# Linear attention and a rational feed-forward layer on one core: attention by pairs of blocks, the state in half-block steps, a newly planned order

## The chip, the core and the metric

The kernel runs on one core of a Trainium2 chip. A core has five engines with a queue of their own each: TensorE (PE in the profile; its weight loads are listed as PEld), VectorE (DVE), ScalarE (ACT), GpSimd (POOL) and SyncE (SP), which here issues the DMA transfers. TensorE writes into PSUM; VectorE and ScalarE read PSUM and SBUF; GpSimd's operands here are all in SBUF. The metric is the device time of one execution in microseconds (us).

## The reference

A recurrence over 768 time steps in 4 batches and 8 heads of width 48, and behind it a feed-forward layer with a rational activation:

```python
for t in range(S):                       # r, k, v: (4, 8, 768, 48)
    cur = einsum('bhd,bhe->bhde', u[None] * k[:, :, t], v[:, :, t])
    y[:, :, t] = einsum('bhd,bhde->bhe', r[:, :, t], state + cur)
    state = w[None, :, :, None] * state + einsum('bhd,bhe->bhde', k[:, :, t], v[:, :, t])
h = x @ w_in                             # x: y as (3072, 384); w_in: (384, 2048)
P = a[0] + a[1]*h + a[2]*h*h + a[3]*h*h*h
Q = 1.0 + abs(b[0])*abs(h) + abs(b[1])*h*h
out = (P / (Q + 1e-6)) @ w_out           # w_out: (2048, 384)
```

## The kernel before

**Attention** is done in 24 blocks of 128 time steps (block n is batch n % 4, steps 128 (n // 4) and on). The decay is divided out: r is scaled by powers of w, k by their inverses (scale_r, scale_k), so that inside a half block of 64 steps the recurrence is a masked product. A block takes these steps. The bonus of the current step is formed by elementwise multiplies and a sum (bonus_a, bonus_b, bonus_sum, bonus_v). k and r are transposed on TensorE (trk_pe, trr_pe, line 415) and copied out of PSUM. a_pe (lines 438 and 439) makes, for each pair of heads p and each half e, two 64x64 products, one from the array's rows 0 to 63 into columns 64 to 127, one from rows 64 to 127 into columns 0 to 63: 16 matmuls a block, all into one PSUM bank. a_ev masks them (line 452). kv_pe (lines 472 and 473) forms the sums of k times v: for the first half block alone over 64 rows, and for both halves together over 128 rows. kv_ev (line 487) adds each to the state carried in, and carry (line 511) decays the state for the next block of the batch. y_pe (line 500) multiplies the r rows and the masked a rows with the state and v rows, 128 rows deep, in two column halves. y_ev adds the bonus, xt_pe (line 519) transposes the result, and xt_hi and xt_lo split it into a high part and a rest.

**The feed-forward layer** works on 12 tiles of two blocks (256 rows). Both weights are split into a high part and a rest once (28 pieces, cv_load to cv_lo, which use ScalarE, VectorE and GpSimd). A product of two split numbers is three matmuls. A tile has eight slices of two 128-column groups of the hidden layer: f1 (mm, line 541) makes 18 matmuls of 256 columns; ew_z, ew_q, ew_t, ew_ln, ew_exp on ScalarE (lines 572 to 592) and ew_u3, ew_hi, ew_p, ew_d, ew_lo on VectorE (lines 596 to 616) give the activation, split again in g: a high part (ew_hi) and a rest (ew_lo); f2 (mm2, lines 545 to 547) makes 12 matmuls of 384 columns. With the last slice cut in two there are 97. The second matmul of a slice waits for ew_lo.

**The order** of every engine's instructions is written out before the program starts. Every step is a task with the engines that may do it, a duration, its dependences, the buffers it takes and a key; run() plays the queues through with these durations, and each time an engine comes free it gives it the ready task with the smallest key. Loads of k, r and v aren't issued before their own time on this clock (AT of the block, less some us). Where TensorE has nothing ready early on, it gets small matmuls on ones (warm, line 1009). Two parameters settle where ew_lo runs: GTIME = 754.72 is the time from which GpSimd may have it, which never comes, so it stays on VectorE; by the same bound the masking stays on VectorE. The planned order is fixed; on the chip each instruction waits for what it needs, and whatever stands behind it on its engine waits too.

Of the kernel before, what the change touches and what calls it, by code (L numbers as in the profile page):

```python
# [30 lines left out]


@with_exitstack
def tile_linear_attention_rational_ffn(ctx, tc, r, k, v, w, u, w_in, w_out, a, b, out):
# [15 lines left out]
    NM = 7  # L50
    NTC = 2
# [32 lines left out]
    w128b = w128.unsqueeze(2).to_broadcast([P, NP, D])  # L84
# [236 lines left out]
    rh, kh, ysa, ysb, vs = ([], [], [], [], [])  # L321
    vs2 = [cst.tile([P, 5, 2, NP, D], F32, name=f"vs{i}") for i in range(B // 2)]
    for i in range(3):
        for lst, nm in ((rh, "rh"), (kh, "kh")):
            lst.append(cst.tile([P, NP, 2, HALF], F32, name=f"{nm}{i}"))
    kt = cst.tile([P, NP, P], F32, name="kt")
    for i in range(2):
        for lst, nm in ((ysa, "ysa"), (ysb, "ysb")):
            lst.append(cst.tile([P, NP, P], F32, name=f"{nm}{i}"))
# [4 lines left out]
    def pro_pad(i):  # L334
        for lst in (rh, kh):
            nc.gpsimd.memset(lst[i][:, :, :, D:HALF], 0.0)

# [16 lines left out]
    def att_load(n, what):  # L354
        bi, i = blk(n)
        c = slice(i * P, (i + 1) * P)
        if what == "v":
            t, src = ld.tile([P, H, D], F32, tag="ldv", name=f"vn{n}"), v
            state[n]["v"] = t
        else:  # L360
            t, src = (hv(kh[n % 3]), k) if what == "k" else (hv(rh[n % 3]), r)
        nc.sync.dma_start(t, src[bi, :, c, :].rearrange("h t d -> t h d"))
# [27 lines left out]
    def scale_r(n, e):  # L390
        rr = hv(rh[n % 3])
        e.tensor_mul(rr, rr, wrn)

    def bonus_a(n, e):
        m = at.tile([P, H, D], F32, tag="m", name=f"m{n}", bufs=NM)
        e.tensor_mul(m, hv(rh[n % 3]), hv(kh[n % 3]))
# [15 lines left out]
    def trans(n, src, nm):  # L412
        p_ = pat(nm, n)
        for p in range(NP):
            nc.tensor.transpose(p_[:, ts(p, P)], src[:, p].rearrange("t a d -> t (a d)"), ident)  # L415
# [5 lines left out]
    def trk_ev(n, e):  # L421
        copy(e, kt.rearrange("p a t -> p (a t)"), state[n]["tk"])

    def trr_pe(n):
        trans(n, rh[n % 3], "tr")

    def trr_ev(n, e, half):
        y_, rows = ((ysa, slice(0, HALF)), (ysb, slice(HALF, P)))[half]
        copy(e, y_[n % 2][rows].rearrange("p a t -> p (a t)"), state[n]["tr"][rows])

    def a_pe(n):
        p_ = pat("a", n)
        ya, yb = ysa[n % 2], ysb[n % 2]
        for p in range(NP):
            for e in range(2):
                c = slice(e * HALF, (e + 1) * HALF)
                o = slice(p * P + e * HALF, p * P + (e + 1) * HALF)
                nc.tensor.matmul(p_[HALF:P, o], kt[0:HALF, p, c], ya[0:HALF, p, c], start=True, stop=True)  # L438
                nc.tensor.matmul(p_[0:HALF, o], kt[HALF:P, p, c], yb[HALF:P, p, c], start=True, stop=True)
        state[n]["a"] = p_  # L440

    def a_rows(n, half):
        return ((ysa[n % 2], slice(HALF, P)), (ysb[n % 2], slice(0, HALF)))[half]


    def a_ev(n, half, e):
        y_, rows = a_rows(n, half)
        av = state[n]["a"][rows]
        if e is nc.scalar:
            copy(e, y_[rows].rearrange("p a t -> p (a t)"), av)  # L450
            return
        nc.vector.tensor_mul(
            y_[rows].rearrange("p a (e t) -> p (a e) t", e=2), av.rearrange("p (c t) -> p c t", t=HALF),
            mask[rows].unsqueeze(1).to_broadcast([HALF, 2 * NP, HALF]),
        )

    def a_mask(n, half):
        y_, rows = a_rows(n, half)
        yv = y_[rows].rearrange("p a t -> p (a t)")
        nc.gpsimd.affine_select(  # L460
            yv, yv, pattern=[[0, 2 * NP], [1, HALF]], base=-1, channel_multiplier=-1,
            compare_op=ALU.is_ge, fill=0.0,
        )

    def kv_pe(n):
        d = state[n]
        p_ = pat("kv", n)
        k_, v_ = kh[n % 3], d["v"]
        pv = p_[:, 0 : 2 * NP * D].rearrange("p (e a d) -> p e a d", e=2, a=NP)
        for e, rows in ((0, slice(0, HALF)), (1, slice(0, P))):  # L470
            for p in range(NP):
                nc.tensor.matmul(pv[0:D, e, p], k_[rows, p, 0, 0:D], v_[rows, 2 * p], start=True, stop=True)  # L472
                nc.tensor.matmul(
                    pv[HALF : HALF + D, 1 - e, p], k_[rows, p, 1, 0:D], v_[rows, 2 * p + 1], start=True, stop=True
                )
        d["kv"] = pv

    def kv_ev(n, e, half):
        bi, i = blk(n)
        s_, pv = vs[bi], state[n]["kv"]  # L480
        outs, prev, rows = ((slice(1, 3), 0, slice(0, D)), (slice(2, 5, 2), 3, slice(HALF, HALF + D)))[half]
        o = s_[rows, outs].rearrange("p e a d -> p e (a d)")
        kv = pv[rows].rearrange("p e a d -> p e (a d)")
        if i == 0:
            copy(e, o, kv)
        else:
            nc.vector.tensor_add(
                o, kv, s_[rows, prev : prev + 1].rearrange("p e a d -> p e (a d)").to_broadcast([D, 2, NP * D])
            )

    def y_pe(n):
# [4 lines left out]
        for p in range(NP):  # L496
            for x, (y_, S_) in enumerate(((ysa[n % 2], SA), (ysb[n % 2], SB))):
                for e in range(2):
                    c = slice(e * HALF, (e + 1) * HALF)
                    nc.tensor.matmul(pv[c, 2 * p + x], y_[:, p, c], s_[:, S_[e], p], start=True, stop=True)  # L500
# [6 lines left out]
    def carry(n, e, half):  # L507
        bi, i = blk(n)
        s_ = vs[bi]
        dst, rows = ((0, slice(0, D)), (3, slice(HALF, HALF + D)))[half]  # L510
        e.tensor_mul(s_[rows, dst], s_[rows, 2], w128b[rows])  # L511
# [32 lines left out]
    def mm2(o, j, hi, lo):  # L544
        nc.tensor.matmul(o, hi, wo_hi[:, j], start=(j == 0), stop=False)  # L545
        nc.tensor.matmul(o, hi, wo_lo[:, j], start=False, stop=False)  # L546
        nc.tensor.matmul(o, lo, wo_hi[:, j], start=False, stop=(j == NJ - 1))  # L547


    SL = [(f, j, JG) for f in range(NTILE) for j in range(0, NJ, JG)]  # L550
    SL[-1:] = [(NTILE - 1, j, 1) for j in range(NJ - JG, NJ)]
    NS = len(SL)

# [84 lines left out]
    def f2(s, hf):  # L638
        f, j0, nj = SL[s]
        if j0 == 0 and hf == 0:  # L640
            ops[f] = [ps_o.tile([P, 512], F32, tag=f"o{x}", name=f"o{f}_{x}") for x in range(2)]
        for jj in range(nj):
            c = ds(jj * N1 + hf * P, P)
            mm2(ops[f][hf][:, 0:DM], j0 + jj, gs[s]["hi"][:, c], gs[s]["lo"][:, c])

    def put_out(f, e, hf):
        bi, i = blk(2 * f + hf)
        os_ = at.tile([P, DM], F32, tag="os", name=f"os{f}_{hf}")
        if e is nc.scalar:
            e.activation(os_, ops[f][hf][:, 0:DM], AF.Copy, scale=SG)  # L650
        else:
            e.tensor_scalar(os_, ops[f][hf][:, 0:DM], SG, None, op0=ALU.mult)
        oss[f, hf] = os_

    def put_dma(f, hf):
# [478 lines left out]
```

## Time and profile before

| what | value |
|---|---|
| time of the runs | 595.18 us median of 3 (594.43 to 595.61) |
| profiled execution | span 593.4 us from its first to its last instruction; its own time is not listed beside the span |
| PE, PEld busy | 563.1 us (95%), 540.8 us (91%) |
| DVE busy | 517.7 us (87%) |
| ACT busy | 435.5 us (73%) |
| POOL busy | 166.5 us (28%) |
| matmuls of f1 (x1728), f2 (x1152) | lines 541; 545, 546 and 547 |
| clock-keeping matmuls | 514, 35.2 us |
| mean granted TensorE clock | 0.984 |

Matmuls overlap in a pipeline, so the duration of one (289 ns for f1's) is more than the time from one start to the next; what a matmul costs is read from the distance of the starts. A float32 matmul of attention shows as two records. The rows of the profile are: line, engine, operation, tiles written and read, shapes, count, then busy time and mean duration, then the idle time of the engine before these instructions and what ended it.

### The profile page before, as it was taken

Reading aid. Unit: us, or ns where it says so; the run is one execution under the profiler, and the core shown is the slowest. Engines: PE = TensorE matmul, PEld = TensorE weight load, DVE = VectorE, ACT = ScalarE, POOL = GpSimd, SP = SyncE. Lnnn points to the kernel's source line nnn. Section 1 sums busy time; section 2 is a strip of 40 time slices with the busy share of each in tenths; the row PEclk is TensorE's granted clock in tenths of the full one; section 3 lists DMA queues with packets and bytes.
Section 4 is the critical chain, followed back from the end, with each engine's and each line's share of the span. In section 5 each row is a group of like instructions: output and inputs, shape, how many; then the busy total and the mean of one; then the engine's idle time right before and its main releaser. Section 6 shows DMA issues by size and latency. Waiting matters only on the chain.

```text
span 593.4 us, 14638 instructions
## 1 busy us (share of the span) xinstructions
PE 563.1 (95%) x5991; PEld 540.8 (91%) x5991; DVE 517.7 (87%) x825; ACT 435.5 (73%) x729; POOL 166.5 (28%) x189
## 2 busy tenths in 40 slices
PE   8899696789999999999999999999999999999995
PEld 8799585778999999999999999999999999999995
DVE  5999998999999997889899888898888998888882
ACT  7679876978862785777677878865778785888780
POOL 6698976664135121013040010143001010000000
PEclk9999888989999999999999999999999999999999
DMA  7687653551222230012020003021003000000000
GB/s 189 163 224 193 166 142 92 127 109 32 55 53 57 68 75 8 2 41 54 28 55 2 27 1 73 10 42 43 14 0 81 2 15 15 0 28 2 28 1 31
DMA packets 95807, 34.85 MB, mean 59 GB/s; under 512 B 89074, under 2 KB 92148, under 8 KB 95732
## 3 DMA queue, kind: packets, MB, share of 16 engines
q1 hardware_dynamic: 95732, 33.83, 23.4%
q8 instruction: 49, 0.80, 0.6%
q14 instruction: 26, 0.21, 0.1%
HBM read 29.11 MB, written 4.72 MB: 57 GB/s over the span
## 4 chain that ended last, share of the span: by engine, by line
PE 71%; DVE 3%; ACT 1%; issue 1%
PE h L541 29%; PE o L545 11%; PE o L546 10%; PE o L547 10%; PE y L500 2%; PE a L438 2%; PE kv L472 2%; PE x L519 1%; PE tk L415 1%; PE tr L415 1%; DVE h L596 1%; DVE q L606 0%; DVE g L602 0%; DVE vs L511 0%; ACT t L583 0%
## 5 line engine op out<-in xcount | busy, mean ns | idle before, releaser
L541 PE MATMUL h<-xth,wi_hi 128*128 128x256 f32 x576 | 166.2, 289 | 0.0
L541 PE MATMUL h<-xtl,wi_hi 128*128 128x256 f32 x576 | 161.6, 281 | 0.0
L541 PE MATMUL h<-xth,wi_lo 128*128 128x256 f32 x576 | 161.5, 280 | 0.0
L545 PE MATMUL o<-wo_hi,g 128*128 128x384 f32 x384 | 134.8, 351 | 0.0
L547 PE MATMUL o<-wo_hi,g 128*128 128x384 f32 x384 | 130.4, 339 | 1.4 <-DVE g L616 1.4
L546 PE MATMUL o<-wo_lo,g 128*128 128x384 f32 x384 | 130.1, 339 | 0.0
L572 ACT ACTIVATE q<-h 128x512 f32<-128x512 f32 (+1 forms) x97 | 57.4, 591 | 83.3 <-PE h L541 63.0
L541 PEld LDWEIGHTS h<-xth,wi_hi 128*128 128x128 f32 x576 | 109.0, 189 | 1.2
L541 PEld LDWEIGHTS h<-xtl,wi_hi 128*128 128x128 f32 x576 | 109.2, 190 | 0.0
L541 PEld LDWEIGHTS h<-xth,wi_lo 128*128 128x128 f32 x576 | 108.8, 189 | 0.0
L602 DVE SCALAR_TENSOR_TENSOR g<-h,sig,z 128x512 fp32r<-128x512 f32 (+1 forms) x97 | 72.0, 743 | 28.1 <-ACT z L592 25.8
L578 ACT ACTIVATE w<-q,off,root 128x512 f32<-128x512 f32 (+1 forms) x97 | 75.8, 781 | 2.9 <-DVE q L606 2.7
L596 DVE SCALAR_TENSOR_TENSOR h<-t,sig,h 128x512 f32<-128x512 f32 (+1 forms) x97 | 72.0, 742 | 3.2 <-ACT t L583 2.9
L583 ACT ACTIVATE t<-h,off,root 128x512 f32<-128x512 f32 (+1 forms) x97 | 74.7, 770 | 0.1
L547 PEld LDWEIGHTS o<-wo_hi,g 128*128 128x128 f32 x384 | 72.6, 189 | 2.4 <-DVE g L616 2.4
L612 DVE SCALAR_TENSOR_TENSOR h<-h,sig,q 128x512 f32<-128x512 f32 (+1 forms) x97 | 72.7, 750 | 2.3
L606 DVE SCALAR_TENSOR_TENSOR q<-w,sig,g 128x512 f32<-128x512 f32 (+1 forms) x97 | 72.1, 743 | 2.6
L545 PEld LDWEIGHTS o<-wo_hi,g 128*128 128x128 f32 x384 | 72.6, 189 | 1.4
L546 PEld LDWEIGHTS o<-wo_lo,g 128*128 128x128 f32 x384 | 72.7, 189 | 0.0
L592 ACT ACTIVATE z<-z,lnb 128x512 f32<-128x512 f32 (+1 forms) x97 | 69.9, 721 | 2.3
L588 ACT ACTIVATE z<-w,lnb 128x512 f32<-128x512 f32 (+1 forms) x97 | 66.4, 685 | 3.6 <-POOL wi_lo L306 1.1
L616 DVE TENSOR_TENSOR g<-h,z 128x512 fp32r<-128x512 f32 (+1 forms) x97 | 65.7, 679 | 0.7
(147 smaller groups left out, 932.0 us busy)
## 6 DMA issues: line engine op xcount, KB each, us to landing
sto<-in_moe_w_out_dram SPq DMA_DIRECT2D x16, 384.0 KB, 3.7
sti<-in_moe_w_in_dram SPq DMA_DIRECT2D x12, 512.0 KB, 5.2
rh<-in_r_dram SPq DMA_DIRECT2D x24, 192.0 KB, 3.7
kh<-in_k_dram SPq DMA_DIRECT2D x24, 192.0 KB, 3.3
vn<-in_v_dram SPq DMA_DIRECT2D x24, 192.0 KB, 3.4
out_dram<-os SPq DMA_DIRECT2D x24, 192.0 KB, 1.9
vs<-in_v_dram SPq DMA_DIRECT2D x24, 96.0 KB, 3.5
wraw<-in_w_dram SPq DMA_DIRECT2D x1, 1.5 KB, 2.3
```

Of the source, the lines that this page charges most:

```text
L541: nc.tensor.matmul(o, wt_[:, cc, ts(j, P)], x_[:, cc], start=(n == 0), stop=(n == 3 * NCC - 1))
L545: nc.tensor.matmul(o, hi, wo_hi[:, j], start=(j == 0), stop=False)
L546: nc.tensor.matmul(o, hi, wo_lo[:, j], start=False, stop=False)
L547: nc.tensor.matmul(o, lo, wo_hi[:, j], start=False, stop=(j == NJ - 1))
L578: nc.scalar.activation(g["w"], w_, AF.Square, scale=RB, bias=KB)
L583: nc.scalar.activation(g["t"], g["h"], AF.Square, scale=RA, bias=KA)
L588: nc.scalar.activation(g["z"], g["w"], AF.Ln, scale=2.0 ** -LN_SHIFT, bias=lnb[:, 2:3])
L592: nc.scalar.activation(g["z"], g["z"], AF.Exp, scale=-1.0, bias=lnb[:, 1:2])
L596: nc.vector.scalar_tensor_tensor(g["h"], g["t"], KAP, g["h"], op0=ALU.add, op1=ALU.mult)
L602: nc.vector.scalar_tensor_tensor(g["hi"], g["h"], c0, g["z"], op0=ALU.add, op1=ALU.mult)
L606: nc.vector.scalar_tensor_tensor(g["q"], g.get("w", g["q"]), qe, g["hi"].bitcast(F32), op0=ALU.add, op1=ALU.mult)
L612: nc.vector.scalar_tensor_tensor(g["d"], g["h"], c0, g["q"], op0=ALU.add, op1=ALU.subtract)
```

## The change

- **a by pairs of blocks.** a_pe takes a pair of blocks (the same steps of two batches; one tile of the feed-forward layer). Its 32 matmuls are 48 rows deep, and consecutive ones go round all four 64x64 quadrants of the array: q, the head of the pair, chooses the rows, e, the half block, the columns. Each row half writes a PSUM bank of its own. The result is masked in four pieces per pair instead of two per block, with the same number of elements.
- **The state per half block in a chain.** kv_pe takes a pair too. Each half block has its own sum, 64 rows deep, in a quadrant; the state at the half block is the state carried in and the first sum, the state at the end is that and the second sum (kv_ev). The product over 128 rows is gone. For the last block of each batch the second sum isn't formed. carry is done once for a pair, over twice the elements.
- **Buffers.** kt and ys hold both blocks of a pair; r has two buffers instead of three; the rows between 48 and 64 of ys are cleared once (pro_rest).
- **The planner** moves out of the kernel to order_of, with a new set of keys and release times (PRM). It knows three modes of the array, a cost for switching between them (TURN) and a bonus MB for staying in one. The first matmul of a slice no longer names pieces of w_out as a dependence; f2 does. Clock-keeping matmuls may be set until 248.69 on its clock (60.0 before), but none after the first f2 has started.
- **The rest's multiply (ew_lo)** goes to GpSimd for the slices listed in SIDE, 20 to 96; ew_d then writes SBUF instead of PSUM for these.
- NT is 1, so the new code for several tiles in turn (NSEG, SEG, opens, closes, partial sums in put_out) leaves the order of slices as it was.

```diff
+PRM = {'AT': (19.16, 39.84, 50.08, 155.58, 173.74, 187.74, 196.43, 217.1, 298.25, 394.8, 423.47, 439.93),
...
+ 'DX': -15.2,
+ 'HFREE': 1,
+ 'MASKED': (),
+ 'MB': 6.1,
+ 'NT': 1,
...
+ 'SIDE': (20, 21, 22, 23, 24, 25, 26, 27, 28, 29, 30, 31, 32, 33, 34, 35, 36, 37, 38, 39, 40, 41, 42, 43, 44, 45, 46, 47, 48, 49,
...
+          80, 81, 82, 83, 84, 85, 86, 87, 88, 89, 90, 91, 92, 93, 94, 95, 96),
+ 'WARM0': 1.6,
+ 'WARM1': 248.69,
...
+TURN = {(0, 0): 0.0, (0, 1): 0.15, (0, 2): 0.15, (1, 0): 0.19, (2, 0): 0.19, (1, 2): 0.2, (2, 1): 0.2, (1, 1): 0.0, (2, 2): 0.0}
...
-    def a_pe(n):
-        p_ = pat("a", n)
-        ya, yb = ysa[n % 2], ysb[n % 2]
-        for p in range(NP):
-            for e in range(2):
-                c = slice(e * HALF, (e + 1) * HALF)
-                o = slice(p * P + e * HALF, p * P + (e + 1) * HALF)
-                nc.tensor.matmul(p_[HALF:P, o], kt[0:HALF, p, c], ya[0:HALF, p, c], start=True, stop=True)
-                nc.tensor.matmul(p_[0:HALF, o], kt[HALF:P, p, c], yb[HALF:P, p, c], start=True, stop=True)
+    def a_pe(m):
+        ps = [pat("a", (m, q)) for q in range(2)]
+        for x in range(2):
+            for p in range(NP):
+                for e in range(2):
+                    c = ts(e, HALF)
+                    for q in range(2):
+                        nc.tensor.matmul(
+                            ps[q][c, ts(x * NP + p, HALF)], kt[RROWS[q], x, p, c], ys[q][RROWS[q], x, p, c], start=True, stop=True
+                        )
...
-    def kv_pe(n):
-        for e, rows in ((0, slice(0, HALF)), (1, slice(0, P))):
...
-                nc.tensor.matmul(pv[0:D, e, p], k_[rows, p, 0, 0:D], v_[rows, 2 * p], start=True, stop=True)
+    def kv_pe(m):
+        last = m // 2 == NB - 1
+        ps = [pat("kv", (m, e)) for e in range(1 if last else 2)]
+        for x in range(2):
+            k_, v_ = hv(kh[(2 * m + x) % 3]), state[2 * m + x]["v"]
             for p in range(NP):
+                for e, p_ in enumerate(ps):
+                    for q in range(2):
+                        nc.tensor.matmul(
+                            p_[RROWS[q], ts(x * NP + p, D)], k_[ts(e, HALF), 2 * p + q], v_[ts(e, HALF), 2 * p + q], start=True, stop=True
+                        )
...
+    def kv_ev(m, q, e, on):
+        s_ = vs2[m % 2][RROWS[q]].rearrange("p e x a d -> p e (x a d)")
+        chain = ((0, 1, 2), (3, 4, 2))[q]
+        pv, dst = state["kv", m, e][RROWS[q]], s_[:, chain[e + 1]]
+        if m < 2 and e == 0:
+            copy(on, dst, pv)
         else:
+            nc.vector.tensor_add(dst, pv, s_[:, chain[e]])
...
+    def carry(m, q, e):
+        s_ = vs2[m % 2][RROWS[q]]
+        e.tensor_mul(s_[:, (0, 3)[q]], s_[:, 2], w128[RROWS[q]].unsqueeze(1).unsqueeze(3).to_broadcast([D, 2, NP, D]))
...
+                tx = t + x * PRM["DX"]
+                add(("Lk", n), lambda e, n=n: att_load(n, "k"), tx - 6, {"S": 1.2}, [w_("kv", (n - 3) // 2), w_("tk", n - 3), w_("ba", n - 3)])
+                add(("Lr", n), lambda e, n=n: att_load(n, "r"), tx - 5.5, {"S": 1.2}, [w_("tr", n - 2), w_("ba", n - 2)])
...
+            side[s] = s in PRM["SIDE"]
+            add(("lo", s), lambda e, s=s: ew_lo(s, e), t + 8, {"G": 0.15 + 1.08 * x} if side[s] else {"D": 0.1 + 0.53 * x}, [("d", s)],
```

More of the change, by code (lines that the diff above doesn't have):

```diff
@@ L324, in tile_linear_attention_rational_ffn @@
         for lst, nm in ((rh, "rh"), (kh, "kh")):
[L325 to L329, printed above, removed]
+            if i < 2 or nm == "kh":
+                lst.append(cst.tile([P, NP, 2, HALF], F32, name=f"{nm}{i}"))
+    kt = cst.tile([P, 2, NP, P], F32, name="kt")
+    ys = [cst.tile([P, 2, NP, P], F32, name=f"ys{q}") for q in range(2)]
+    RROWS = (slice(0, D), slice(HALF, HALF + D))
+    AROWS = (slice(HALF, P), slice(0, HALF))
     for i in range(B):
@@ L334, in pro_pad, with pro_rest @@
     def pro_pad(i):
-        for lst in (rh, kh):
+        for lst in (rh, kh)[i == 2 :]:
             nc.gpsimd.memset(lst[i][:, :, :, D:HALF], 0.0)
+    def pro_rest(q):
+        nc.gpsimd.memset(ys[q][slice(32, HALF) if q == 0 else slice(P - 32, P)], 0.0)
     def pro_state(i, e):
@@ L478, in kv_ev @@
[L478 to L485, printed above, removed]
-        else:
-            nc.vector.tensor_add(
-                o, kv, s_[rows, prev : prev + 1].rearrange("p e a d -> p e (a d)").to_broadcast([D, 2, NP * D])
-            )
+        trans(n, rh[n % 2], "tr")
@@ L496, in y_pe @@
         for p in range(NP):
-            for x, (y_, S_) in enumerate(((ysa[n % 2], SA), (ysb[n % 2], SB))):
+            for q, S_ in enumerate((SA, SB)):
                 for e in range(2):
-                    c = slice(e * HALF, (e + 1) * HALF)
-                    nc.tensor.matmul(pv[c, 2 * p + x], y_[:, p, c], s_[:, S_[e], p], start=True, stop=True)
+                    c = ts(e, HALF)
+                    nc.tensor.matmul(pv[c, 2 * p + q], ys[q][:, n % 2, p, c], s_[:, S_[e], p], start=True, stop=True)
         state[n]["y"] = pv
@@ L777, in build @@
+        lastf = {SL[s][0]: s for s in range(NS)}
         for s in range(NS):
@@ L797, in build @@
             for hf in range(2):
[L798 to L805 removed]
+                first = opens(s)
@@ new lines, in build @@
+                new = [("o", ("o", s))] if first and hf == 0 else []
+                so = max(s_ for s_ in range(s + 1) if SL[s_][0] == f and opens(s_))
+                wo_ = [("co", p0 + 3 + (j0 + jj) % 4) for jj in range(nj)]
+                prev = ("f2", s, 0) if hf else ("f2", s - 1, 1) if s else None
+                add(("f2", s, hf), lambda e, s=s, hf=hf: f2(s, hf), t + 5.5 + hf * 0.1, {"P": 1.06 * x}, [("lo", s), prev, *wo_],
+                    new=new, use=[("g", s)] + ([] if new else [("o", so)]), cols=2304 * x)
@@ new lines, in build @@
+                if closes(s):
+                    done = j0 + nj == NJ
+                    some = so > min(s_ for s_ in range(NS) if SL[s_][0] == f)
+                    buf = ("os", f, hf)
+                    prv = [("os", max(s_ for s_ in range(s) if SL[s_][0] == f and closes(s_)), hf)] if some else []
+                    add(("os", s, hf), lambda e, s=s, hf=hf: put_out(s, hf, e), t + 6, {"D": 0.53} if some else {"A": 0.37, "D": 0.53}, [("f2", s, hf), *prv],
+                        new=[] if some else [("os" if done else "m", buf)], use=[("o", so)] + ([buf] if some else []))
+                    if done:
+                        add(("od", f, hf), lambda e, f=f, hf=hf: put_dma(f, hf), t + 7, {"S": 0.6}, [("os", s, hf)], use=[buf])
@@ L813, in prologue @@
         for i in range(3):
-            add(("pad", i), lambda e, i=i: pro_pad(i), 0.1, {"G": 0.3})
+            add(("pad", i), lambda e, i=i: pro_pad(i), 0.1, {"G": 0.2})
+        for q in range(2):
+            add(("rest", q), lambda e, q=q: pro_rest(q), 0.2, {"G": 1.0})
         add(("msk",), lambda e: pro_mask(), 3, {"G": 0.9}, [("pl",)])
```

654 lines of the change are left out of this document (352 added, 302 removed), and 6 rows, old and new, of the table OFF.

## The prediction

> **What bounds the kernel now.** I read the page's span and engine shares first, then the busy time by stretch, then TensorE's instructions in order of time.
>
> ```profile
> span 593.4 us, 14638 instructions
> PE 563.1 (95%) x5991; PEld 540.8 (91%) x5991; DVE 517.7 (87%) x825; ACT 435.5 (73%) x729; POOL 166.5 (28%) x189
> ```
>
> ```profile
> 0.00:20.00 20.00, 17.08 (x261) 16.47 (x262) 12.88 (x19) 13.09 (x26) 13.51 (x29) 1.00 0.84 219
> 20.00:140.00 120.00, 100.82 (x1585) 91.32 (x1585) 112.41 (x197) 96.16 (x180) 87.46 (x85) 0.93 0.57 141
> 140.00:200.00 60.00, 58.75 (x643) 55.16 (x639) 56.25 (x90) 39.99 (x71) 21.87 (x25) 1.00 0.25 51
> 200.00:585.00 385.00, 384.80 (x3506) 376.54 (x3505) 335.56 (x521) 285.70 (x453) 43.65 (x51) 1.00 0.11 26
> 585.00:594.00 9.00, 1.61 (x10) 1.29 (x8) 0.62 (x1) 0.58 (x1) 0.00 (x0) 0.87 0.15 50
> ```
>
> The columns are the stretch, its length, the busy time of PE, PEld, DVE, ACT and POOL, the granted clock, and the DMA share and rate. There are two regimes. From 140 to 585 TensorE is full (58.75 of 60, then 384.80 of 385): 445 us in which only less TensorE work shortens anything. Before 140 TensorE's busy share is partly clock-keeping matmuls, and VectorE is the full one: 112.4 of 120 us, 94%, with ScalarE at 96.2 (80%). The tail of 8.4 us is the last eviction and store. So 593.4 = 140 (start, VectorE) + 445 (TensorE) + 8.4.
>
> How much attention already lies in the start is told by the groups of TensorE before 140:
>
> ```profile
> L473 PE MATMUL kv<-vn,kh 128*48 128x48 f32 (+1 forms) x176 | 11.8, 214 | 0.0
> ...
> L438 PE MATMUL a<-ysa,kt 64*64 64x64 f32 x160 | 11.8, 221 | 3.5 <-ACT ysb L309 2.3 <-DVE bitso L295 1.1
> ```
>
> A block has 16 records on each of these lines (eight matmuls, two records each), so 11 blocks have had kv and 10 have had a: some 10.3 blocks of 24 are done by 140, and 13.7 are left for the full part.
>
> **The change, part by part.** *Quadrants.* What one attention step costs TensorE in the full part I take as the time from the last ordinary matmul before it to the second one after it, less two ordinary steps.
>
> ```profile
> 276.69 0.28 PE L541 MATMUL h<-xtl,wi_hi 128*128 128x256 f32 x1
> 276.81 0.28 PE L541 MATMUL h<-xth,wi_lo 128*128 128x256 f32 x1
> ...
> 277.12 0.22 PE L439 MATMUL a<-ysb,kt 64*64 64x64 f32 x1
> ...
> 277.94 0.22 PE L439 MATMUL a<-ysb,kt 64*64 64x64 f32 x1
> 278.09 0.39 PE L541 MATMUL h<-xth,wi_hi 128*128 128x256 f32 x1
> 278.31 0.28 PE L541 MATMUL h<-xtl,wi_hi 128*128 128x256 f32 x1
> ...
> 306.88 0.29 PE L500 MATMUL y<-vs,ysb 128*64 128x48 f32 x4
> ...
> 307.58 0.29 PE L500 MATMUL y<-vs,ysb 128*64 128x48 f32 x4
> ...
> 309.85 0.34 PE L547 MATMUL o<-wo_hi,g 128*128 128x384 f32 x1
> ...
> 310.21 0.20 PE L473 MATMUL kv<-vn,kh 64*48 64x48 f32 x1
> 310.25 0.20 PE L472 MATMUL kv<-vn,kh 64*48 64x48 f32 x1
> ...
> 310.48 0.20 PE L473 MATMUL kv<-vn,kh 64*48 64x48 f32 x1
> 310.61 0.24 PE L472 MATMUL kv<-vn,kh 128*48 128x48 f32 x1
> ...
> 311.39 0.34 PE L546 MATMUL o<-wo_lo,g 128*128 128x384 f32 x1
> ```
>
> For a: 278.31 - 276.81 = 1.50, less two steps of 0.12 (276.69 to 276.81), is 1.26 us. Inside, the two diagonal quadrants run as a pair: 14 pairs from 277.12 to 277.94, 0.0586 us each, so 16 pairs are 0.94 and entering and leaving the mode costs the other 0.32. For kv: 311.39 - 309.85 = 1.54, less two steps of 0.176 (a 384-column step is 1.5 times the 256-column one), is 1.19; six pairs from 310.21 to 310.48 give 0.045, 16 pairs 0.70 to 0.72, and the rest is entry, exit and the switch in the middle (310.48 to 310.61, 0.13 where a pair takes 0.045).
>
> The new kernel issues for a pair of blocks 64 records of a and 64 of kv, spread over all four quadrants. No row shows four quadrants at once. The bounds are: four together (16 groups at the pair's pace: a 0.94, kv 0.70 a pair) and two together as now (a 1.89, kv 1.41). I take four, for this reason: the pace of a pair goes with the stationary columns and not with the moving ones. y streams 48 columns against 64 stationary ones and needs (307.58 - 306.88) / 12 = 0.058 a pair, like a; kv streams 48 against 48 and needs 0.045. So loading weights sets the pace, and the partners' instructions come within 0.01 to 0.04 of each other (310.21, 310.25 is already the next pair), which leaves room for two more. With entry and exit of 0.3, a pair of blocks costs 1.24 for a instead of 2.52 and 1.00 for kv instead of 2.38: 2.66 a pair, 1.33 a block. (The last state of each batch isn't formed any more: under 1 us, left out.)
>
> The page "TensorE: Matmul & The Clock Gate" of the Trainium skill, section "Wait — 56ns, not 53.3ns?", says that start-to-start never drops below about 25 ns however small the matmul is; by it 64 records would take 1.6 us for a as for kv, little better than two together. The rows just shown already average 22 ns for kv, so the trace speaks against that floor between different tiles.
>
> *y, transposes, x* keep their counts. y's two blocks can follow one another, and kv and a can too, each time saving an entry of 0.3: at most 24 times (7 us), at least never; I take 4 us.
>
> *The low product to GpSimd.* The new list of slices 20 to 96 puts the low half's multiply on GpSimd for 77 slices.
>
> ```profile
> L616 DVE TENSOR_TENSOR g<-h,z 128x512 fp32r<-128x512 f32 (+1 forms) x97 | 65.7, 679 | 0.7
> L306 POOL TENSOR_TENSOR wi_lo<-bitsi,wi_hi x7: 1292/1298/1687, 37.4 to 108.2; 128x512 fp32r<-128x512 f32 x7
> ```
>
> VectorE loses 77 x 0.679 = 52 us; GpSimd, by its nearest multiply-like instruction of that shape, gains 77 x 1.30 = 100 us on top of 21.87 + 43.65 = 66 after 140, 37% of the full part. Neither engine bounds there, so this is worth nothing by itself. It lengthens the chain to the second matmul by 1.30 - 0.68 = 0.62 a slice. What hides it is that TensorE works on the next slice's first matmul meanwhile (two times nine steps of 0.117, 2.1 us). Without that cover it costs 77 x 0.62 = 48 us.
>
> *The order.* The new release keys hold back the loads of the fourth pair until 155.58 - 15.2 - 6 = 134 of the planner's clock, so six blocks lie in the start where 10.3 lie now. That takes 4.3 blocks out of the VectorE-bound stretch. Attention's work on VectorE in 20 to 140 is 18 groups, from the first to the last here, together 62.2 us or 6.0 a block:
>
> ```profile
> L487 DVE TENSOR_TENSOR vs<-kv,vs 48x384 f32<-48x384 f32 x14 | 7.7, 552 | 0.6 <-PE kv L473 0.4
> ...
> L401 DVE TENSOR_TENSOR m<-m,ub 128x384 f32<-128x384 f32 x1 | 0.7, 655 | 0.0
> ```
>
> 4.3 x 6.0 / 0.94 = 27 us: by VectorE the start could end at 113. ScalarE bounds it next: its 96.2 us at the same 94% are 102, so 122 if no work of its own went away; some does. I take 115, between 113 and 125. The 4.3 blocks come back in the full part at the new price: a and kv 1.12, y 1.24 (0.94 and 0.3), and 11 transposes at about a 256-column step each, 1.3 (an estimate): 3.6 a block, 15.5 us. Their 26 us on VectorE are paid out of the 52 that GpSimd took over; with that cover gone, VectorE, at 56.25 of 60 us in 140 to 200, would bound there.
>
> *The rest* costs nothing: one carry per pair instead of two of half the size, the same evictions and masks in other groupings, the clock-keeping matmuls only where TensorE is idle. With one r buffer fewer, a load of r waits on SyncE's queue for the block before the last; behind it stand weight loads in the start and stores later. A load lands in 3.7 us, and in the full part a block comes only every 445 / 18 = 25 us, which hides it; were it not hidden, it would be 3.7 a block at the most, 67 us.
>
> ```profile
> rh<-in_r_dram SPq DMA_DIRECT2D x24, 192.0 KB, 3.7
> ```
>
> **Sum**, on the profiled execution's span: full part 445 - 13.7 x 1.33 + 15.5 - 4 = 438; start 115; tail 8.4: 562. The runs shown have a median of 595.18, 1.8 above the span; I add 1.8: 563. With the start at 113 to 125 and 0 to 7 for shared entries this case runs from 556 to 577; I call 552 to 576 its own range, for the stretches that a new order can still pack better.
>
> **Rivals.**
> (a) *Only two quadrants at a time* (the change not doing what it says). Then a block saves (2.38 - 1.71 + 2.52 - 2.19) / 2 = 0.5 instead of 1.33, and 18 blocks in the full part are 15 us dearer: 578. For it: no row shows four. Against it: the close starts of partners. By that page of the Trainium skill, with its floor of 25 ns, the time would be about this one too.
> (b) *The start is packed much better.* If conversion alone sets it and it ends near 98, the time is 546. For it: ScalarE is idle for 24 us of the 120. Against it: weights, attention and first slices compete for three engines, all above 70%.
> (c) *Slower: GpSimd is late with the low product.* Its queue is in order, and attention's multiplies stand in it, waiting for loads:
>
> ```profile
> POOL kh L388 <- DMA kh<-in_k_dram: 68.8, 3, 38.0
> ```
>
> Now such waits hurt nobody; with a low product behind one, the slice's second matmul waits, and after one slice of lookahead TensorE stops. Where the chain is exposed at all 77 slices it costs the 48 us above: 611. It is slower than before from 32 / 0.62 = 52 exposed slices on, or by a few waits of the 38-us kind. Against it: GpSimd is 63% idle there, and the order puts an instruction behind a load only when it is expected to have landed.
> (d) *No change*: (a) holds, and the start ends at 133 although it holds six blocks only. The full part is then 445 - 13.7 x 0.5 + 4.3 x 4.4 - 4 = 453, and 453 + 133 + 8.4 + 1.8 = 596.
>
> **How the numbers follow.** The forecast has 0.58, (a) and its like between 576 and 588 have 0.17, (b) 0.11, (c) 0.11, (d) 0.03. A difference of 0.2% (1.2 us) is about what a measurement of this kernel tells from none; the three runs shown differ by that. Faster 0.86, same 0.03, slower 0.11. The range goes from 546, the price of (b), to 586, above (a): about 0.05 lies below and 0.14 above.
>
> **What would show it.** Quadrants: a pair of blocks' 64 records of a from first to last start in about 0.95 us, of kv in 0.7; with (a) they take 1.9 and 1.4. Order: fewer than 8 blocks of kv before TensorE is full, which should begin between 110 and 125. Low product: 77 GpSimd multiplies near 1.3 us, DVE near 465 us in all, and waits of the second matmul for it under 5 us in total; (c) shows as tens of us there. The prediction is wrong if TensorE has gaps after 130, or if its step for the ordinary matmuls (0.117) is no longer kept because something else paces it.

## The result, and the profile after

The changed kernel takes 574.43 us (median of 4 runs, 573.96 to 575.17) where the kernel before takes 594.80 beside it (594.00 to 595.61): a ratio of 0.966, with a 95% interval of 0.9646 to 0.9674, so 20 us less. The forecast was 563. The profiled execution's span is 572.5 us.

The page of the changed kernel: the span, the busy times, and the chain of work that ended last by engine.

```profile
span 572.5 us, 14798 instructions
...
PE 536.9 (94%) x6006; PEld 519.1 (91%) x6006; DVE 461.0 (81%) x713; ACT 443.5 (77%) x735; POOL 267.7 (47%) x256
...
PE 57%; DVE 19%; ACT 12%; issue 5%; POOL 2%; DVEq 0%; ACTq 0%; POOLq 0%
```

VectorE lost 57 us of work (517.7 to 461.0), GpSimd gained 101, and TensorE has 26 us less busy time. In the chain TensorE carries 57% (71% before), and VectorE and ScalarE together 31% (4% before): TensorE isn't the only limit any more. Where the others carry it, the busy time by stretch says (columns as in the prediction):

```profile
20.00:115.00 95.00, 80.56 (x1333) 75.07 (x1332) 83.19 (x139) 78.23 (x144) 71.34 (x64) 0.96 0.50 136
115.00:120.00 5.00, 5.00 (x29) 5.00 (x28) 3.73 (x7) 3.83 (x8) 2.03 (x2) 0.66 0.02 3
120.00:180.00 60.00, 59.87 (x488) 58.95 (x487) 53.94 (x82) 54.49 (x89) 13.08 (x13) 1.00 0.21 46
180.00:260.00 80.00, 73.84 (x1280) 69.10 (x1279) 75.23 (x118) 49.43 (x87) 49.41 (x48) 1.00 0.36 73
260.00:565.00 305.00, 302.67 (x2735) 298.44 (x2734) 233.07 (x348) 243.54 (x380) 116.94 (x100) 1.00 0.13 31
565.00:573.00 8.00, 2.39 (x14) 2.07 (x12) 0.00 (x0) 1.10 (x2) 0.12 (x1) 0.96 0.17 59
```

TensorE is full from 115 on, as forecast. But from 180 to 260 it has 6 us of holes, and VectorE is the full one there: 75.23 of 80, 94%. In this stretch lie the masks of five pairs, 3 to 7, so 10 of the 18 blocks that were left for the full part; the other eight lie further on. First and last of the five, and TensorE's four longest waits in the stretch (total us, times, longest):

```profile
L689 DVE TENSOR_TENSOR ys<-a(3, 0)_2823,mask 64x512 f32<-64x512 f32 x2 | 1.4, 690 | 0.0
...
L689 DVE TENSOR_TENSOR ys<-a(7, 1)_3811,mask 64x512 f32<-64x512 f32 x2 | 1.4, 688 | 0.0
```

```profile
PE x L746 <- DVE m L734: 1.5, 2, 0.9
PE tr L653 <- POOL vs L738: 1.5, 2, 0.8
PE tk L653 <- DVE ys L689: 1.2, 1, 1.2
PE y L729 <- DVE ys L689: 0.8, 2, 0.4
```

In the kernel before, the same view of the same stretch has a single line:

```profile
PE a L438 <- ACT ysb L309: 0.5, 1, 0.5
```

Now attention itself waits, on masks and on the bonus added to y. The row that names the carry is the profile's inference: tr, the transpose of r, doesn't read what the carry writes, so what released it there is not shown.

The four quadrants work as costed. In order of time, the matmuls of a for pair 3:

```profile
181.58 0.27 PE L675 MATMUL a(3, 0)_2823<-ys,kt 48*64 48x64 f32 x1
181.58 0.27 PE L675 MATMUL a(3, 1)_2824<-ys,kt 48*64 48x64 f32 x1
181.59 0.27 PE L675 MATMUL a(3, 0)_2823<-ys,kt 48*64 48x64 f32 x1
...
182.52 0.22 PE L675 MATMUL a(3, 1)_2824<-ys,kt 48*64 48x64 f32 x1
```

Four start within 0.02 us, and 64 records go from 181.58 to 182.52: 0.94 us, the number of the prediction. kv has two tiles for a pair, with 32 records each on both:

```profile
L705 PE MATMUL kv(3, 0)_2757<-vn,kh x32: 205/205/240, 177.4 to 178.1; 64*48 64x48 f32 x32
L705 PE MATMUL kv(3, 1)_2758<-vn,kh x32: 205/205/240, 177.4 to 178.1; 64*48 64x48 f32 x32
```

That is 0.7 us for 64, also as costed. And the low product on GpSimd is not late:

```profile
L854 POOL TENSOR_TENSOR g<-q,z 128x512 fp32r<-128x512 f32 (+1 forms) x77 | 99.4, 1291 | 193.4 <-DVE q L850 173.9
...
L774 PE MATMUL o<-wo_hi,g 128*128 128x384 f32 x384 | 130.4, 339 | 3.8 <-DVE g L854 3.8
```

77 products of 1.29 us (1.30 was the estimate), and the second matmul waited 3.8 us in all for a low product, and then for those that stayed on VectorE.

**Where 11 us are missing.** The prediction's sum has a full part of 438 us, from 115 to 553. It lasts 450, from 115 to 565. What a block costs in it can be had from the counts of ordinary matmuls, at the prediction's steps of 0.117 and 0.176 us. Up to 140 the kernel before, and up to 115 the changed one, had done this many (each row is one of the three lines of f1 and f2; the other two have the same count, but for one f2 line of the changed kernel with 23):

```profile
L541 PE MATMUL h<-xth,wi_hi 128*128 128x256 f32 x54 | 17.0, 315 | 0.0
...
L545 PE MATMUL o<-wo_hi,g 128*128 128x384 f32 x20 | 8.1, 404 | 0.0
```

```profile
L768 PE MATMUL h<-xth,wi_hi 128*128 128x256 f32 x48 | 13.9, 290 | 0.5 <-DVE q L844 0.3 <-ACT ys L542 0.2
...
L774 PE MATMUL o<-wo_hi,g 128*128 128x384 f32 x22 | 7.9, 361 | 3.8 <-DVE g L854 3.8
```

Before: 1728 - 162 of f1 and 1152 - 60 - 10 (tail) of f2 are 183.2 + 190.4 = 373.6 us, so 445 - 373.6 = 71.4 us for 13.7 blocks, 5.2 a block. After: 1728 - 144 and 1152 - 67 - 14 are 185.3 + 188.5 = 373.8, so 76.2 us for 18 blocks, 4.2 a block. The forecast had 438 - 373.8 = 64.2, 3.6 a block. The 12 us between 76.2 and 64.2 are the error (the end behind TensorE's last full stretch is 1 us shorter than the 8.4 of before). By the rows above, TensorE is idle for 8.6 of them (0.1 + 6.2 + 2.3); without these gaps a block costs 3.75. So most of the error is waiting, and little of it is TensorE's own work. The experiments ask why.

### The profile page after: what moved, and what is told of

Read it like the earlier page. It is cut to its first block, busy times and chain, and to the rows that moved or that the text cites. A ratio compares the mean times of both kernels' runs of the same rounds, so it can differ in the third digit from the quotient of the medians.

```text
span 572.5 us, 14798 instructions
## 1 busy us (share of the span) xinstructions
PE 536.9 (94%) x6006; PEld 519.1 (91%) x6006; DVE 461.0 (81%) x713; ACT 443.5 (77%) x735; POOL 267.7 (47%) x256
## 4 chain that ended last, share of the span: by engine, by line
PE 57%; DVE 19%; ACT 12%; issue 5%; POOL 2%; DVEq 0%; ACTq 0%; POOLq 0%
PE h L768 24%; PE o L772 9%; PE o L773 9%; PE o L774 9%; DVE ys L689 3%; DVE g L840 2%; DVE vs L718 2%; DVE h L834 2%; PE y L729 2%; ACT t L821 2%; ACT z L826 2%; DVE q L844 1%; ACT q L810 1%; ACT w L816 1%; DVE ys L542 1%
## 5 line engine op out<-in xcount | busy, mean ns | idle before, releaser
L854 POOL TENSOR_TENSOR g<-q,z 128x512 fp32r<-128x512 f32 (+1 forms) x77 | 99.4, 1291 | 193.4 <-DVE q L850 173.9
L768 PE MATMUL h<-xth,wi_hi 128*128 128x256 f32 x576 | 164.2, 285 | 0.5 <-DVE q L844 0.3
L768 PEld LDWEIGHTS h<-xth,wi_hi 128*128 128x128 f32 x576 | 108.5, 188 | 1.6 <-ACT ys L542 0.5
L850 DVE SCALAR_TENSOR_TENSOR q<-h,sig,q 128x512 f32<-128x512 f32 (+1 forms) x77 | 57.1, 742 | 1.9
```

The source lines that it names most:

```text
L768: nc.tensor.matmul(o, wt_[:, cc, ts(j, P)], x_[:, cc], start=(n == 0), stop=(n == 3 * NCC - 1))
L854: e.tensor_mul(g["lo"], g["d"], g["z"])
```

## The experiments

All times are medians, and ratios are to the kernel before, run on the same chip.

**Two quadrants at a time.** e becomes the outer loop in a_pe and kv_pe, so that neighbours in the order share a column half.

```diff
-        for x in range(2):
-            for p in range(NP):
-                for e in range(2):
+        for e in range(2):
+            for x in range(2):
+                for p in range(NP):
...
-        for x in range(2):
...
-            for p in range(NP):
-                for e, p_ in enumerate(ps):
+        for e, p_ in enumerate(ps):
+            for x in range(2):
...
+                for p in range(NP):
```

> The changed kernel with the loops of a and kv reordered so that the half block e is outermost: consecutive matmuls then go round two quadrants instead of four, with the same matmuls, buffers and order of steps. Theory (four quadrants run at once and TensorE bounds the part behind the start): a costs 0.95 us and kv 0.70 us more for each pair of blocks, and the nine pairs behind the start make 15 us: 587 to 591. Rival (VectorE bounds the stretches in which attention is done, so TensorE's time there is covered): 574 to 578.

577.87 us, 0.9723 (0.9694 to 0.9751): only some 3.5 us more, and the rival is right. The price on TensorE did rise:

```profile
L675 PE MATMUL a(3, 0)_2823<-ys,kt x32: 218/218/267, 182.9 to 184.6; 48*64 48x64 f32 x32
...
L705 PE MATMUL kv(3, 0)_2757<-vn,kh x32: 205/205/240, 178.2 to 178.9; 64*48 64x48 f32 x32
L705 PE MATMUL kv(3, 1)_2758<-vn,kh x32: 205/205/240, 178.8 to 179.5; 64*48 64x48 f32 x32
```

a takes 1.69 us instead of 0.94, 6.8 us over nine pairs. kv's two tiles now follow one another, 1.30 us instead of 0.73, 4.0 us over the seven of these pairs that have both. That is 10.8 us in all. Most of it went into holes that were there anyway: in 180 to 260 TensorE's busy time went up and VectorE's down, and TensorE's idle time behind 120 fell from 8.6 to 3.6 us.

```profile
180.00:260.00 80.00, 78.50 (x1280) 74.53 (x1279) 72.96 (x118) 48.61 (x86) 50.97 (x49) 1.00 0.38 75
```

**The low product back on VectorE**, at its place in the order:

```diff
-                fns[n_](ENG.get(e))
+                fns[n_](ENG.get("D" if n_[0] == "lo" else e))
```

> The changed kernel with the low product of slices 20 to 96 on VectorE again, at the same place in the written-out order (ew_d still writes SBUF). Theory (VectorE has no room where attention is done): 77 x 0.69 = 53 us more on VectorE; the quiet stretches take it, the stretches with attention don't, so 580 to 592. Rival (VectorE is 81% busy and has 110 us to spare): 573 to 577.

581.06 us, 0.9768 (0.9744 to 0.9793): 6.5 us more, at the theory's low end. VectorE's busy time rises by 41 us (461.0 to 502.2) and not by the 53 that were expected: the 77 products take 56.0 us there, and its other instructions together 15 us less. The profile shows where the time goes:

```profile
180.00:260.00 80.00, 70.03 (x1251) 65.12 (x1250) 78.15 (x124) 45.42 (x80) 38.35 (x38) 1.00 0.36 71
```

VectorE is at 98% in the stretch of the five pairs, and TensorE falls from 73.84 to 70.03.

**The low product on GpSimd in the kernel before**, for the slices from 20 on, in the old order:

```diff
-                tasks[n_]["fn"](ENG.get(e))
+                on_g = n_[0] == "lo" and n_[1] >= 20
+                if n_[0] == "d":
+                    side[n_[1]] = n_[1] >= 20
+                tasks[n_]["fn"](ENG.get("G" if on_g else e))
```

> The kernel before, with only the low product of slices 20 to 96 put on GpSimd at its place in the old order. Theory (the old full part is bounded by TensorE, so relief of VectorE alone brings nothing): 594 to 598. Rival (this move is the gain, whatever the order): under 585.

596.08 us, 1.0013 (0.9999 to 1.0026). VectorE lost 44 us of work (517.7 to 473.9) and the time did not move, as the theory had it.

**The squares later.** The step whose two-column multiply took 5.42 us in the changed kernel (last section) is moved to just before the first mask.

```diff
     bank.update(tag_of)
+    late = order.pop(order.index((("sq",), "D")))
+    order.insert(next(i for i, (n_, e) in enumerate(order) if n_[0] == "ae"), late)
```

> The changed kernel with pro_squares (some fifteen tiny VectorE instructions) moved in the order from behind the second r copy to just before the first mask. In the changed kernel's trace the multiply of two columns on line 373 takes 5.42 us, from 18.59 until GpSimd's run of back-to-back instructions ends at 23.99. Theory (it waits for GpSimd, and the start is late by it): the multiply takes under 1 us, and 4 to 5 us go from the time: 569 to 571. Rival (the loads set the start): 574.

577.33 us, 0.9695 (0.9671 to 0.972): 2 us more, if anything, and not less, so neither text had it. The multiply itself fell to 0.16 us, but another instruction took over its wait (last section).

**Where VectorE's work costs time.** Two kernels leave out about the same amount of VectorE's work, each in another place: most of the masks of the five pairs, and most of a product of 25 slices in the quiet part.

```diff
+        nc_ = 1 if 3 <= m <= 7 else 2 * NP
-        on.tensor_mul(a_out(q, e), av, mask[ts(e, HALF)].unsqueeze(1).to_broadcast([HALF, 2 * NP, HALF]))
+        on.tensor_mul(a_out(q, e)[:, 0:nc_], av[:, 0:nc_], mask[ts(e, HALF)].unsqueeze(1).to_broadcast([HALF, nc_, HALF]))
```

> Left out: for pairs 3 to 7 (the ten blocks that the changed kernel does between 177 and 250 us) the mask multiply is done over one of its eight groups of columns, so 20 instructions of 0.69 us should take about 0.15: some 11 us less work on VectorE, all of it between 180 and 260 us, where VectorE is busy 75.23 of 80; nothing changes on TensorE. Theory (VectorE bounds this stretch, and that is where the gain went): the time falls by 7 to 11 us, to 563 to 567, and TensorE's holes in 180 to 260 (6 us idle by its busy time, more by its useful work) shrink. Rival (the stretch is bound by the chain of turns, copies and carries from engine to engine, and VectorE is only busy beside it): the time falls by 0 to 4 us, to 570 to 574.

```diff
-        nc.vector.scalar_tensor_tensor(g["d"], g["h"], c0, g["q"], op0=ALU.add, op1=ALU.subtract)
+        d, h, q = (g[x][:, 0:128] if s in range(36, 61) else g[x] for x in "dhq")
+        nc.vector.scalar_tensor_tensor(d, h, c0, q, op0=ALU.add, op1=ALU.subtract)
```

> Left out: for slices 36 to 60 (done between about 270 and 390 us, where no pair but one is due) the subtraction that ends in d, 0.749 us for 128x512, is done over 128 of its 512 columns: 25 instructions that should take about 0.3, some 11 us less work on VectorE, as much as burst_masks_narrow takes away, in another place: 260 to 400 us, where VectorE is busy 104 of 140 and TensorE 139. Theory (VectorE's work costs time only where the blocks come together): no change, 573 to 576. Rival (VectorE's total of 461 us, or the length of the chain of products of each slice, sets the time): the time falls by as much as with the masks, 4 to 11 us, to 563 to 570.

With the narrow masks 569.91 us, 0.9579 (0.9561 to 0.9597); with the narrow products 573.26, 0.9639 (0.962 to 0.9657), whose interval overlaps that of the changed kernel. The groups in question, and the stretch they lie in, first the masks:

```profile
L690 DVE TENSOR_TENSOR ys<-a(3, 0)_2823,mask 64x64 f32<-64x64 f32 x2 | 0.4, 222 | 0.0
...
180.00:260.00 80.00, 77.39 (x1312) 73.12 (x1310) 71.12 (x125) 53.53 (x92) 52.59 (x50) 1.00 0.37 75
```

and the products:

```profile
L851 DVE SCALAR_TENSOR_TENSOR q<-h,sig,q 128x128 f32<-128x128 f32 x25 | 8.7, 350 | 0.7
...
260.00:400.00 140.00, 139.37 (x1157) 138.12 (x1156) 95.82 (x151) 115.59 (x177) 50.86 (x42) 1.00 0.14 32
```

20 x (0.69 - 0.22) = 9.3 us less in the burst gave about 4.8 us; 25 x (0.75 - 0.35) = 10 us less elsewhere gave nothing that can be told from none. So the place counts, not VectorE's total. But 4.8 lies between the two theories' numbers: half of the work that was left out came back as time, so VectorE's own work is only a part of what holds the stretch up.

**Half of these masks off VectorE**, with all the work done: a copy on ScalarE and a select on GpSimd in their place.

```diff
     bank.update(tag_of)
+    moved = [("ae", m, q, 1) for m in range(3, 8) for q in range(2)]
+    for n_ in moved:
+        i = order.index((n_, "D"))
+        order[i : i + 1] = [(n_, "A"), (("am", *n_[1:]), "G")]
+        fns[("am", *n_[1:])] = lambda e, n_=n_: a_mask(*n_[1:])
```

> All the work is done. Half of the masks of pairs 3 to 7 (ten multiplies of 0.69 us, 6.9 us of VectorE) become a copy on ScalarE at the same place in the order (0.6 us each; ScalarE is busy 49 of 80 us in 180 to 260) and a select on GpSimd right behind it (estimate 0.8 us each from 0.89 to 1.3 us for the larger products there; GpSimd is busy 49 of 80). Theory (VectorE bounds the stretch): 569 to 572. Rival (the hand-over to GpSimd, two steps where there was one, puts the products and the select behind GpSimd's other work and eats the gain): 574 to 580.

580.21 us, 0.974 (0.9714 to 0.9767): 5 us more, at the upper end of the rival's range. Part of it goes with the clock: four of the six runs, at a mean granted clock of 0.98, took 580 to 581 us, and the two at 0.99, like the changed kernel's, took 577.2 and 577.5, 3 us more than it. The stretch (with a granted clock of 0.94 in this profile, 1.00 in the changed kernel's), and what TensorE and VectorE waited for in it:

```profile
180.00:260.00 80.00, 71.61 (x1234) 67.04 (x1233) 66.29 (x103) 49.38 (x87) 55.34 (x57) 0.94 0.35 71
```

```profile
PE x L746 <- DVE m L734: 3.1, 1, 3.1
PE y L729 <- POOL ys L693: 1.8, 2, 1.4
```

```profile
DVE m L734 <- PE y L729: 4.3, 4, 2.4
DVE dt L644 <- POOL m L639: 3.9, 2, 2.7
```

VectorE is busy for 9 us less and idles: y waits for GpSimd's select, VectorE waits for y and for GpSimd's bonus products. By these waits the stretch is held up by the chain from engine to engine, in which VectorE is the busiest link, and a longer chain costs more than the relief brings.

**Another order.** All the work is done, but the planner gets other keys, release times and a few other durations, and its rule on shared operands is changed: a VectorE step that reads two SBUF operands (the list SHARED, now with the squares and the last power) is taken to stand still until GpSimd pauses. Its core (the release times rounded):

```diff
-PRM = {'AT': (19.16, 39.84, 50.08, 155.58, 173.74, 187.74, 196.43, 217.1, 298.25, 394.8, 423.47, 439.93),
+PRM = {'AT': (11.81, 40.83, 67.69, 135.91, 144.63, 157.15, 194.93, 275.38, 275.55, 336.83, 349.22, 451.66),
...
+            if e == "D" and t["shared"] and idle["G"] > now + 1e-9:
+                idle["D"], held = 1e9, i
+                continue
...
-    SHARED = {"sk", "sr", "ba", "bb", "bv", "ca", "co", "LV", "ch"}
+    SHARED = {"sq", "wl", "sk", "sr", "ba", "bb", "bv", "ca", "co", "LV", "ch"}
```

> All the work is done, with the same instructions; only the order is another one. The pairs are aimed at 12, 41, 68, 136, 145, 157, 195, 275, 275, 337, 349 and 452 us, so that four of the ten blocks of the burst lie before 180 us and four behind 260, the low product is on GpSimd for 47 of 97 slices, and 17 of the 48 masks go through ScalarE and GpSimd. Theory (the gain was lost because the blocks come together where VectorE then bounds): about 560 to 570. Rival (the blocks cost the same wherever they are put in the part that TensorE fills): 573 to 585; an order that is not made for the times of this chip can also lose, so a time above 575 alone doesn't speak against the theory unless VectorE is under 90% in every stretch.

562.65 us, 0.9451 (0.9423 to 0.9478), better than both kernels: 32 us less than before, 12 less than the changed kernel.

```profile
span 560.5 us, 14837 instructions
...
120.00:180.00 60.00, 58.46 (x744) 55.87 (x743) 55.77 (x87) 48.31 (x83) 32.76 (x35) 1.00 0.42 87
180.00:260.00 80.00, 80.00 (x903) 78.79 (x902) 65.93 (x101) 63.70 (x104) 25.36 (x25) 1.00 0.13 30
260.00:552.00 292.00, 290.91 (x2822) 286.68 (x2821) 242.97 (x374) 231.46 (x374) 79.45 (x75) 1.00 0.16 36
552.00:561.00 9.00, 3.43 (x20) 3.10 (x18) 0.51 (x2) 1.11 (x2) 0.00 (x0) 0.81 0.15 52
```

The lines of this file are numbered some 110 higher. Up to 115 it has done 52, 51 and 51 of f1's three matmuls, 24 of each of f2's, and three pairs, hardly more than the changed kernel:

```profile
L878 PE MATMUL h<-xth,wi_hi 128*128 128x256 f32 x52 | 15.0, 288 | 3.1 <-DVE q L960 1.6 <-ACT kt L652 0.9 <-DVE q L954 0.6
...
L882 PE MATMUL o<-wo_hi,g 128*128 128x384 f32 x24 | 10.0, 416 | 0.0
```

The full part goes from 115 to 552, 437 us; 1574 of f1 and 1060 of f2 are 184.2 + 186.6 = 370.8, which leaves 66.2 for 18 blocks, 3.7 a block. That is close to the 3.6 that the prediction gave a block, and TensorE's idle time in it is 2.6 us (1.5 + 0 + 1.1) instead of 8.6.

**The same prices in both orders.** Is it the spreading that gives each quadrant its worth? The two orders with dearer attention products: two quadrants at a time, and, with some of these matmuls written twice, about the old price.

```diff
+        sets = [(e, x, p) for e in range(2) for x in range(2) for p in range(NP)]
+        for e, x, p in sets + sets[0:6]:
...
+        sets = [(e, x, p) for e in range(len(ps)) for x in range(2) for p in range(NP)]
+        for e, x, p in sets + sets[0:8]:
```

> The changed kernel's order, with the attention products at about the old price: a and kv two quadrants at a time, and a part of them written a second time (6 of 16 sets for a, 8 of 16 for kv), so that a pair costs TensorE some 2.6 us more than with four quadrants (old 2.52 + 2.38 = 4.90 a pair, new 1.24 + 1.00 = 2.24); nine pairs lie behind 120 us: 23.5 us. Theory (the holes of the burst hide the first part of that price, 6 of 9.6 us with two quadrants, and TensorE bounds beyond): 23.5 - 6 = 17.5, so 589 to 594. Rival (something else than TensorE bounds the burst, so the price is hidden in the same proportion, 3.5 of 9.6): 581 to 585.

> The new order of replanned, with a and kv two quadrants at a time: the same 9.6 us more on TensorE behind 120 us that cost the changed kernel 3.5. Theory (where the blocks do not come together, no hole hides TensorE's work, and the quadrants are worth their whole price): 569 to 573. Rival (the price is hidden as before): 564 to 567.

> The order of replanned, with the attention products at about the old price as in old_price: 2.6 us more a pair, nine pairs behind 120 us, 23.5 us. Theory (whole price, less a few us that the start and 120 to 180 hide): 582 to 587. Rival (hidden in part as in the burst): 570 to 578.

| products of attention | changed kernel's order | other order |
|---|---|---|
| four quadrants | 574.43, 0.966 | 562.65, 0.9451 |
| two quadrants | 577.87, 0.9723 (+3.7 us) | 571.79, 0.9598 (+8.7 us) |
| about the old price | 591.29, 0.9945 (+17.0 us) | 585.51, 0.9833 (+22.7 us) |

(The differences are those of the ratios, times 595; the intervals of the last three ratios are 0.9928 to 0.9961, 0.9585 to 0.961 and 0.982 to 0.9846.) By the distances of its starts in the traces, the nine pairs cost TensorE 10.8 us more with two quadrants and 21.1 more at about the old price (a takes 2.22 and kv 1.89 us a pair, where four quadrants take 0.94 and 0.73); the expectations had 9.6 and 23.5.

In the other order 8.7 of the 10.8 are paid, and 22.7 for the 21.1. That more than the whole is paid goes with the start, whose three pairs are dearer too: by 120 it has done 144 matmuls of f1 and 71 of f2 where four quadrants leave time for 178 and 84, a difference of 6.3 us.

In the changed kernel's order 3.7 of the first 10.8 are paid, and the next 10.3 are paid whole (13.3, of which the rest isn't accounted for). TensorE's idle time behind 120 falls from 8.6 to 3.6 us with two quadrants and then no further (3.4 at the old price). So of the 7 us that stay hidden, 5 go into gaps of TensorE, most of them in the burst, as the stretch of the five pairs shows with the old price.

```profile
180.00:260.00 80.00, 78.79 (x1570) 74.62 (x1570) 70.58 (x113) 46.16 (x82) 48.60 (x47) 1.00 0.38 75
```

**The low product on VectorE in the other order**, with the same edit as above, for its 47 slices:

> The order of replanned with the low product of its 47 slices back on VectorE, at its place in the order: 47 x 0.68 = 32 us more on VectorE (466 before) and 47 x 1.3 = 61 less on GpSimd; no work is left out. Theory (VectorE is the second limit: in 260 to 400 us it is busy 121 of 140, so that there the products come too late for TensorE): 6 to 14 us longer, 569 to 577. Rival (with the blocks apart VectorE has room): 562 to 566.

567.19 us, 0.9527 (0.9514 to 0.954): 4.5 us more, between the theory's range and the rival's. Four pairs' stretch with the product on GpSimd, and then with it on VectorE:

```profile
260.00:400.00 140.00, 138.91 (x1613) 135.44 (x1612) 121.19 (x183) 110.99 (x183) 51.42 (x52) 1.00 0.24 51
```

```profile
260.00:400.00 140.00, 136.55 (x1597) 133.06 (x1596) 124.11 (x192) 109.50 (x182) 34.56 (x38) 1.00 0.25 54
400.00:500.00 100.00, 99.61 (x846) 98.72 (x845) 87.49 (x143) 79.37 (x125) 7.46 (x7) 1.00 0.10 24
```

Here the price isn't paid in one burst: in 260 to 400, where four pairs lie, TensorE falls to 136.55 of 140 (138.91 with the product on GpSimd), in 400 to 500 it stays at 99.6. These 2.4 us are half of the price; for the rest, the start has done 171 matmuls of f1 and 77 of f2 by 120 where it had done 178 and 84, 2.1 us less of ordinary work.

## Why the prediction was right, and where it was off

- **What bounds before** holds: 44 us less on VectorE in the old order changed nothing (1.0013).
- **The quadrants' price** was right in all its numbers: four together, 0.94 and 0.70 inside. Rival (a), two at a time, is excluded by the records; as an experiment it gives 577.87, and the prediction's 578 for it was made of other parts (a full part without the burst), so that agreement is luck.
- **Their worth** was forecast at 13.7 x 1.33 = 18.2 us, with the rest of the 18 blocks' saving inside their price of 3.6. With about the old price the changed kernel is 17.0 slower, of the 21.1 that nine pairs cost TensorE. In the other order it is 22.7, a part of it in the start.
- **The start** was right in its end: TensorE is full from 115, three pairs lie before, and the deferral of 4.3 blocks is what the keys did. The way there was in part luck: VectorE lost 29 us of work in the start (112.4 to 83.2) where 26 were taken, but was busy 88% of 20 to 115 and not the 94% of the sum, by which the start would have ended at 108.5 (20 + 83.19 / 0.94). Rival (b), an end near 98, is not what happened.
- **The low product**: "worth nothing by itself" is right in the old order. In the changed kernel's order it is worth 6.5 us, and the prediction named the condition: with that cover gone, VectorE would bound. Rival (c) is excluded: TensorE waited 3.8 us for low products in all, none of them GpSimd's.
- **What failed is the price at which the deferred blocks come back.** "3.6 a block, 15.5 us" is TensorE's own price, and it rests on two steps: that a block comes "every 445 / 18 = 25 us", and that its VectorE work is "paid out of the 52 that GpSimd took over". Both are means over 445 us. In truth ten blocks come within 80 us, one every 8; in that stretch GpSimd does only ten low products (the row below), which takes 10 x 0.68 = 7 us off VectorE, while ten blocks at the prediction's 6.0 bring 60. VectorE is 94% busy, TensorE waits for attention's steps on other engines, and the price is 4.2 a block. 18 x 0.65 = 12 us, less the 1 us at the end, is the whole error (574.4 against 563). The prediction had named the sign of it: gaps of TensorE after 130 would show it wrong, and 8.6 us of the 12 are such gaps. With the blocks spread, the same work has 3.7 a block and 562.65, so the other terms of the sum hold together; not each of them is confirmed by it. The release times that make the burst stand in the diff: five of twelve between 155 and 217. GpSimd's low products in 180 to 260:

```profile
L854 POOL TENSOR_TENSOR g<-q,z 128x512 fp32r<-128x512 f32 x10 | 13.5, 1349 | 11.8 <-DVE q L850 6.5 <-DMA vn<-in_v_dram 4.1 <-ACT kt L542 1.2
```

- **What stays open.** Taking 9.3 us of the burst's work off VectorE gave half of it back, and moving masks to other engines lost, so VectorE alone doesn't hold that stretch up; which link of the chain is next wasn't settled. VectorE's busy time there also holds waits for GpSimd: three multiplies by dt take 1.12 us each, against 0.55 undisturbed. The other order differs from the changed kernel in more than the spread (17 of 48 masks on ScalarE and GpSimd, 47 low products on GpSimd instead of 77, the rule for SBUF operands); that the spread is the cause rests on the prices being paid nearly in full there and on TensorE's gaps being gone, not on the time alone. The 4 us for shared entries were not measured alone; the trace has 15 of them behind 115 (y's two blocks follow one another in nine pairs, kv and a in six), and at the 0.3 of the prediction that would be 4.5.

## What to carry to other kernels

When work is taken off the stage that is full and put into another one, price it at the density at which it arrives there, not at that stage's mean: an engine with 19% to spare over 450 us can still bound the 80 us into which ten blocks are packed. A cheaper instruction on the bounding engine is worth its price only where nothing else is next in line, so read busy times over stretches as short as the bursts; raising one price in two orders shows how much of it is hidden in each. Moving work to an idle engine within a tight chain can lose, since the chain gets a link longer.

## What the runs showed of the hardware

**Four 64x64 quadrants run at once at the pace of two.** 64 records of a in 0.94 us are 14.7 ns a record, and 64 of kv in 0.73 us are 11.4. A matmul has two records here, so that is 29 and 23 ns a matmul on average, but four matmuls start within 0.02 us. The prediction set the page "TensorE: Matmul & The Clock Gate" of the Trainium skill beside this (section "Wait — 56ns, not 53.3ns?", a floor of about 25 ns from start to start); between matmuls in different quadrants the measurement differs, and it decides.

**A VectorE instruction with two SBUF operands can wait for a whole row of GpSimd instructions.** VectorE and GpSimd in order of time, in the changed kernel:

```profile
18.59 5.42 DVE L373 TENSOR_TENSOR half<-half,ctmp 128x2 f32<-128x2 f32 x1
```

```profile
17.88 0.99 POOL L389 TENSOR_TENSOR ur<-ur,wr 1x384 f32<-1x384 f32 x1
18.84 1.29 POOL L539 TENSOR_TENSOR wi_lo<-bitsi,wi_hi 128x512 fp32r<-128x512 f32 x1
...
22.98 1.01 POOL L630 TENSOR_TENSOR rh<-rh,wrn 128x384 f32<-128x384 f32 x1
```

A multiply of two columns, 0.16 us where it is undisturbed, takes 5.42 us and ends at 24.01, just behind the last of six GpSimd instructions (22.98 + 1.01 = 23.99) that follow each other from 17.88 without a gap. Five of them began after the multiply had (18.59). With the squares later, that multiply takes 0.16, and another instruction with two SBUF operands waits instead:

```profile
23.03 4.17 DVE L648 TENSOR_TENSOR m<-vn,dt 128x384 f32<-128x384 f32 x1
...
31.15 0.16 DVE L373 TENSOR_TENSOR half<-half,ctmp 128x2 f32<-128x2 f32 x1
```

So moving it moved the wait. The time rose by some 2 us in the start, which has done 147 matmuls of f1 by 120 where the changed kernel has 162, a difference of 1.8 us; why isn't shown. The page "SBUF — State Buffer" of the Trainium skill, section "SBUF: two separate sides", says that whichever of the two starts first holds the shared port pair for its whole instruction and the other blocks fully. The trace agrees that VectorE blocks; but the wait here is as long as GpSimd's unbroken run, 5.42 us, not one instruction (1.0 to 1.3).
